# One stretch of small matmul tiles per turn: gated linear attention followed by a gated SSM on one core

## The chip, the cores and the metric

The kernel runs on one core of a Trainium2 chip. The metric is the device time of one execution in microseconds (us), as the median of several runs. TensorE is called PE below (PEld for its weight loads), VectorE DVE, ScalarE ACT, GpSimd POOL and SyncE SP, as in the profile.

## The reference

Two blocks follow each other, all in float32: attention with a recurrent state, gated per channel (4 batches, 8 heads, 768 steps, head size 48), and a gated state-space block (384 in, 512 inside, 384 out).

```python
for t in range(S):                                   # attention, per batch and head
    state = alpha[t][:, None] * state + outer(k[t], v[t])
    y[t] = q[t] @ state
x = y.transpose(0, 2, 1, 3).reshape(B, S, H * D)     # (4, 768, 384)

proj = x @ w_in                                      # (384, 1024)
val, gate = proj[..., :512], proj[..., 512:]
a = exp(A_log)[0]
for t in range(S):
    h = a * h + val[:, t];  ys[:, t] = h
out = (silu(gate) * ys) @ w_out                      # (512, 384)
```

## The kernel before

The 768 steps of a batch are cut into groups of 256 steps; there are N = 12 groups, numbered over the batches. A loop runs over n = 0 to 11. In turn n the kernel does the second block of group n and works ahead on the attention of the groups n+1 and n+2, and on the input of group n+3. The order of the instructions on every engine is the order of the program text (`manual_schedule`); each engine works through its own queue in that order and waits, by semaphores, for the others. So where a call stands in the loop decides what an instruction waits behind.

For a group m the steps are these.

- **products(m)**, seven steps on DVE, handed out one at a time by `go(count)`: transpose the raw alpha (`al`), transpose k, the running product P (a scan over 1028 elements), then ratio, reciprocal and the reverse scan V, then Zk = k * V, then transpose q, then Zq = q * P. The raw tiles `raw_a`, `raw_k`, `raw_q` come by DMA from SP's queue (`load_raw`), one buffer each.
- **scores(m)**: 64 matmuls on 64 x 64 tiles of PE (L798), Zk against Zq, into two pairs of PSUM banks, one pair for each half of the group.
- **masks(m)**: DVE multiplies half of the scores by a triangular mask into `A0` (L813), ACT copies the other half into `AK` (L814) and the keys into `K0` (L820), and POOL masks `AK` in place (L818).
- **values(m, across)** (L834): the masked scores times v, into the bank pair y. It is called twice, once for one diagonal (`across`), once for the other.
- **carried(m, us)** (L847): the state before each quarter of the group times Zq, into the same y.
- **states(m)** (L866): what each quarter adds to the state; ACT copies it to `dS` (L874), and **add_up(m)** lets POOL add it to the running `sum` tiles (L886).
- **join(m)**: ACT copies y to SBUF (L960, L961), SP and POOL issue four DMAs each that move the heads into place in xT (L963), and ACT copies the parts that stand in place already (`rest`, L966).
- **project(n, cc)**, four times per turn: twelve matmuls on the full 128 x 128 array (L988), six for the values into one bank (pv) and six for the gates into a second (pg); DVE scans pv (`hh`, L995), ACT makes silu of pg (L1006), POOL multiplies the two (L1008).
- **output_parts(n)**: the product with w_out as seven half-size products of sums (L1064, 28 matmuls on the full array) into four banks pa, pd, pc, pb. It is a generator with stops. ACT copies partial results (L1072), DVE adds them up (L1091, which reads pb; L1092, which reads pd; L1093, which reads pc), POOL adds the last quarter (L1089, L1094), and SP stores the rows (L1096). `sum_early` and `sum_late` (L1055 to L1060) make the sums of inputs.

PSUM has eight banks. Four (mm0 to mm3) are handed out by a string of digits, `taken`, one digit for each call of `bank()`; two (s0, s1) are for the scores and states, and two (y0, y1) for y. A bank is free again when the last engine that reads it is done.

In a turn of the middle part PE's order is: values(n+1, across) and states(n+1) are first, for which the scores were made in the turn before; then the four projections; then carried and the second values of group n+1; scores(n+2); the output products of group n; and the next turn begins. In the turns after n = 1 and 3 (`late`) scores, values and states stand elsewhere: after the output products, and between the projections. So PE goes to and fro between small and full tiles several times per turn.

While the kernel runs, it also tests whether the inputs lie in the range that this fast path can compute (`check_w`, `check_end`, `check_flag`); the flag is loaded by all engines near the end, and a branch takes a slower general path if it is not set. With the inputs of the reference the fast path's last part runs (L1373).

Of the kernel before, what the change touches and what calls it, by code (L numbers as in the profile page):

```python
# [9 lines left out]
FP32 = mybir.dt.float32  # L10
# [3 lines left out]
AF = mybir.ActivationFunctionType  # L14
# [332 lines left out]
def fast(  # L347
# [22 lines left out]
    nc = tc.nc  # L370
# [104 lines left out]
    AK = const.tile([C, G, 4, D + L], FP32, name="AK")  # L475
    As, Ks = [A0, AK[:, :, :, D:]], [K0, AK[:, :, :, 0:L]]
    Zqs = [const.tile([C, 2 * G, 4, L + D], FP32, name=f"Zq{i}") for i in range(2)]
# [183 lines left out]
    def products(m):  # L661
# [20 lines left out]
    taken = iter("0321032103231023" "1023102310231023" "102310231023" "10"  # L682
                 "23012301" "230132" "02130213" "023101" "23012301" "230132" "01230123" "012310"
                 "23012301" "230132" "01230123" "012310" "23012301" "230132" "01230123" "012310"
                 "23012301" "0132" "01320132")

    def bank(tag=None):
        if tag:
            return ps_at.tile([C, 512], FP32, tag=tag, name=tag)
        return ps_mm.tile([C, 512], FP32, tag=f"mm{next(taken)}", name="mm")  # L690

# [109 lines left out]

    def masks(m, cs=range(G), between=None):
        sc = [[t[:, 0:4 * (L + D)].rearrange("p (h x) -> p h x", h=4) for t in pair] for pair in scs[m]]
        mb = mask[:, None, :]
        if m < NG:
            for c in cs:
                for i in range(2):
                    nc.vector.tensor_mul(As[i][:, c], sc[c][i][:, :, D:], mb.to_broadcast([C, 4, L]))
                for i in range(2):
                    nc.scalar.activation((K0, dS[m % 2][1])[i][:, c, :, 0:D], sc[c][i][:, :, 0:D], AF.Copy)  # L810
            return
        for c in range(G):
            nc.vector.tensor_mul(A0[:, c], sc[c][0][:, :, D:], mb.to_broadcast([C, 4, L]))  # L813
            nc.scalar.activation(AK[:, c], sc[c][1], AF.Copy)  # L814
        if between:
            between()
        t = AK.rearrange("p c h x -> p (c h) x")[:, :, D:]
        nc.gpsimd.tensor_mul(t, t, mb.to_broadcast([C, G * 4, L]))  # L818
        for c in range(G):
            nc.scalar.activation(K0[:, c, :, 0:D], sc[c][0][:, :, 0:D], AF.Copy)  # L820

    def values(m, across):

        v_sb = vs[m % NV]
        if across:
            ys[m] = [t.rearrange("p (e t) -> p e t", e=2) for t in bank_pair("y")]
        for c in range(G):
            for e in range(2):
                for h in range(2):
                    i = 1 - h if across else h  # L830
                    for s in range(2):
                        p = 2 * e + (s ^ i)
                        rows = ds(L * h, L)
                        nc.tensor.matmul(ys[m][i][ds(64 * s, 64), e, ds(c * C + h * L, L)],  # L834
                                         v_sb[rows, c, 4 * i + p, :], As[i][rows, c, p, :],
                                         start=across and c == 0 and e == 0, stop=False, skip_group_check=True)
# [14 lines left out]
    def states(m):  # L851
# [7 lines left out]
        for c in range(G):  # L859
            for p in range(4):  # L860
                for h in range(2):
                    if c < n[h]:
                        rows = ds(L * h, L)
                        for i in range(2):
                            to = st[h][ds(64 * i, D), c, p, :] if m else st[h][c][ds(64 * i, D), p, :]
                            nc.tensor.matmul(to, ((K0, dS[m % 2][1]) if m < NG else Ks)[i][rows, c, p, 0:D],  # L866
                                             wide[rows, c, ds(2 * D * (4 * i + p), D)] if m == 0 else
# [199 lines left out]
    def output_parts(n):  # L1067
# [8 lines left out]
        product(pd, S3, T3, True)  # L1076
        yield
        copy(s7, pd)
# [96 lines left out]

    def second(m):
        if m < N:
            values(m, True)
            states(m)
            add_up(m, (0, 1, 2))  # L1180

    def third(m):
        if m < N:
            carried(m, (1,))
            values(m, False)
            carried(m, (0, 2, 3))
            return join(m, [nc.sync, nc.gpsimd])

    late = (1, 3)
    for n in range(N):  # L1190
# [37 lines left out]
        elif n == 1:  # L1228
# [28 lines left out]
            scaled_k(3, tk, V)  # L1257
            f2()
            output(0)
            sum_weights()  # L1260
# [4 lines left out]
            scaled_q(3, tq, P)  # L1265
            f3()
            go(1)
        else:
            if n == 2:
                first(m)  # L1270
            if n - 1 not in late:
                go(1)
                if n == N - 2:
                    check_w(5)
                next(outs, None)
                second(m)
                go(1)
                if n == N - 2:
                    check_w(0)
            else:  # L1280
                go(2 if n == 2 else 1)
            f0 = project(n, 0)
            f0()
            if n == N - 2:
                check_w(1)
            if n == 2:
# [8 lines left out]
            if n - 1 in late:  # L1295
                second(m)
            if n == 4:
                go(1)
            if n == N - 2:
                check_w(2)  # L1300
# [5 lines left out]
            go(1)  # L1306
            load_raw("q", n + 3, nc.sync)
            f3 = project(n, 3)
# [8 lines left out]
            if n < N - 1:  # L1317
                outs = output_parts(n)
            if n not in late and m + 1 < N:
                scores(m + 1)  # L1320
                masks(m + 1, between=lambda: next(outs))
                if m >= NG:
                    rest()
                    add_up(m, (3,))
                next(outs)
                go(1)
                if n == N - 3:
                    check_w(4)
            else:
                if m < N and m >= NG:  # L1330
                    rest()
                    add_up(m, (3,))
                if n < N - 2:
                    go(1)
                    for _ in outs:
                        pass
            load_v(m + 2, nc.sync)
        if n == N - 2:
            check_flag()
        if n == N - 1:  # L1340
            tc.mark_branch_hint_location("last", hint=0, engines=[mybir.EngineType.PE, mybir.EngineType.Activation, mybir.EngineType.DVE, mybir.EngineType.SP, mybir.EngineType.Pool])
            value = nc.values_load(flag[0:1, 0:1], min_val=0, max_val=1)
        if n == 1:
            output(n)
        if n == N - 2:
            for _ in outs:
                pass
        if n > 1 and n in late:
            first(m + 1)
# [62 lines left out]
```

## Time and profile before

| | |
|---|---|
| median of 3 runs | 274.02 us (273.98 to 274.11) |
| the profiled execution | 274.39 us, of which the span of instructions is 272.7 us |
| busy: PE / PEld / DVE / ACT / POOL | 265.9 / 230.3 / 234.7 / 111.5 / 161.6 us |
| granted PE clock | 0.999 |
| projections, L988 | 576 matmuls, 129.7 us |
| output products, L1064 | 252 matmuls (108 + 72 + 36 + 36), 51.7 us |
| DMA | 41.19 MB, mean 151 GB/s |

The page gives for each engine how long it was busy and how many instructions it had. A matmul of this kernel appears twice, as the load of the weights (PEld) and as the product (PE). In a timeline each row has the start in us from the beginning of the span, the length in us, the engine, the line, the operation, what it writes and reads, the shapes and the count of merged instructions; in brackets stands how long the engine was idle before it, and what ended that. A row of the windows has, for a stretch of time, its length and the busy time and instructions of PE, PEld, DVE, ACT and POOL, then the granted clock, the DMA engines' share and GB/s.

### The profile page before, as it was taken

What the parts mean: (1) busy time and instruction counts of PE and PEld (TensorE: products, weight loads), DVE (VectorE), ACT (ScalarE), POOL (GpSimd) and SP (SyncE); (2) the same over time, 40 slices, a digit from 0 to 9 for tenths busy, and PEclk for the clock granted to TensorE, in tenths of its full rate; (3) what the DMA queues carried; (4) which work ended last, traced back from release to release, by engine and by line L of the source; (5) the groups of instructions that cost most, each with busy time, mean ns of one, the idle gap of its engine ahead of it and who ended that gap; (6) DMA issues with size and microseconds to landing.
All of it is one profiled execution on the core that took longest, in us unless ns stands there. A gap on an engine that the chain in (4) does not pass through costs nothing.

```text
span 272.7 us, 9967 instructions
## 1 busy us (share of the span) xinstructions
PE 265.9 (97%) x4168; PEld 230.3 (84%) x4168; DVE 234.7 (86%) x316; ACT 111.5 (41%) x270; POOL 161.6 (59%) x185
## 2 busy tenths in 40 slices
PE   8999999999998999999999999999999999999995
PEld 6988888877786888888988988988988889888874
DVE  6979998996899999699999998999998998882430
ACT  3767766462341631441542433524525515214111
POOL 8122323175116997689985995996876976646000
PEclk9999999999999999999999999999999999999999
DMA  6937984998692669396588479595587501201101
GB/s 185 308 123 239 295 188 154 241 194 208 195 219 72 139 158 226 94 232 160 113 213 174 103 193 196 118 242 143 138 206 158 139 2 31 75 0 46 60 7 58
DMA packets 52304, 41.19 MB, mean 151 GB/s; under 512 B 27392, under 2 KB 50944, under 8 KB 52256
## 3 DMA queue, kind: packets, MB, share of 16 engines
q1 hardware_dynamic: 49328, 37.34, 55.2%
q0 software_dynamic: 1536, 2.20, 3.0%
q10 hardware_dynamic: 1392, 0.99, 1.2%
q8 instruction: 34, 0.56, 0.9%
q14 instruction: 14, 0.11, 0.2%
HBM read 32.54 MB, written 4.72 MB: 137 GB/s over the span
## 4 chain that ended last, share of the span: by engine, by line
PE 82%; DVE 10%; issue 2%; ACT 2%; DMA 1%; POOL 1%; DVEq 0%; ACTq 0%; POOLq 0%
PE mm L988 42%; PE mm L1064 15%; PE y L834 4%; PE y L847 4%; PE mm L1022 4%; PE mm L798 3%; PE s L798 3%; PE s L866 3%; DVE P L635 2%; PE mm L1373 2%; DVE V L654 2%; PE mm L707 1%; DMA raw_a<-in_alpha_dram 1%; DVE hh L995 1%; DVE k L600 1%
## 5 line engine op out<-in xcount | busy, mean ns | idle before, releaser
L988 PE MATMUL mm<-xT,w_in 128*128 128x256 f32 x576 | 129.7, 382 | 0.8 <-DVE hh L995 0.7
L988 PEld LDWEIGHTS mm<-xT,w_in 128*128 128x128 f32 x576 | 107.8, 190 | 16.9 <-DVE hh L995 1.1
L1006 ACT ACTIVATE sg<-mm 128x256 f32<-128x256 f32 x48 | 18.4, 384 | 89.2 <-PE mm L988 84.2
L1008 POOL TENSOR_TENSOR f_last<-sg,hh 128x256 f32<-128x256 f32 x36 | 30.2, 845 | 30.6 <-ACT sg L1006 21.7
L886 POOL TENSOR_TENSOR sum<-sum,dS 128x192 f32<-128x192 f32 x30 | 38.3, 1276 | 3.7 <-ACT dS L874 2.3
L635 DVE TENSOR_TENSOR_SCAN P<-al,lower 128x1028 f32<-128x1028 f32 x12 | 30.1, 2510 | 0.3
L995 DVE TENSOR_TENSOR_SCAN hh<-a_dec,hh,mm 128x256 f32<-128x256 f32 x32 | 23.4, 730 | 8.0 <-PE mm L988 7.7
L654 DVE TENSOR_TENSOR_SCAN V<-al,ends 128x1028 f32<-128x1028 f32 x12 | 29.3, 2439 | 0.4
L963 POOL DMA_DIRECT2D xT<-yst x44 | 22.5, 516 | 4.6 <-ACT yst L960 3.2
L556 POOL TENSOR_TENSOR w_in<-w_in,wr 128x768 int32<-128x768 int32 x4 | 7.3, 1823 | 25.9 <-DVE wr L551 16.1
L1064 PE MATMUL mm<-wide,wr 128*128 128x192 f32 x108 | 20.5, 326 | 0.0
L600 DVE STREAM_TRANSPOSE k<-raw_k 128x1024 f32<-128x1024 f32 x9 | 18.4, 2049 | 0.0
L600 DVE STREAM_TRANSPOSE q<-raw_q 128x1024 f32<-128x1024 f32 x9 | 18.2, 2025 | 0.0
L1064 PEld LDWEIGHTS mm<-wide,wr 128*128 128x128 f32 x108 | 18.0, 190 | 0.0
L818 POOL TENSOR_TENSOR AK<-AK,mask 128x512 f32<-128x512 f32 x9 | 13.4, 1494 | 7.7 <-ACT AK L814 7.6
L874 ACT ACTIVATE dS<-s 128x384 f32<-128x384 f32 (+1 forms) x18 | 7.4, 461 | 23.8 <-PE s L866 23.8
L619 DVE TENSOR_TENSOR Zk<-k,V 128x1024 f32<-128x1024 f32 (+1 forms) x14 | 16.5, 1181 | 0.1
L600 DVE STREAM_TRANSPOSE al<-raw_a 128x1024 f32<-128x1024 f32 x8 | 16.4, 2051 | 0.0
L1064 PE MATMUL mm<-w_out,f_last 128*128 128x192 f32 x72 | 15.8, 342 | 0.1
L610 DVE TENSOR_TENSOR Zq<-q,P 128x1024 f32<-128x1024 f32 (+1 forms) x14 | 15.2, 1087 | 0.0
L847 PEld LDWEIGHTS y<-Zq,sum 48*64 48x64 f32 x656 | 11.7, 134 | 3.9 <-issue 2.5
L834 PEld LDWEIGHTS y<-AK,v 64*64 64x64 f32 x352 | 12.1, 134 | 2.9 <-issue 2.9
(188 smaller groups left out, 503.4 us busy)
## 6 DMA issues: line engine op xcount, KB each, us to landing
v<-in_v_dram SPq DMA_DIRECT2D x22, 192.0 KB, 3.3
out_dram<-o_sb SPq DMA_DIRECT2D x22, 192.0 KB, 2.7
raw_k<-in_k_dram SPq DMA_DIRECT2D x18, 184.0 KB, 4.7
raw_q<-in_q_dram SPq DMA_DIRECT2D x18, 184.0 KB, 4.3
raw_k<-in_k_dram SPq DMA_DIRECT2D x18, 176.0 KB, 5.0
raw_q<-in_q_dram SPq DMA_DIRECT2D x18, 176.0 KB, 4.7
wbits<-in_moe_w_in_dram SPq DMA_DIRECT2D x8, 384.0 KB, 5.4
raw_a<-in_alpha_dram SPq DMA_DIRECT2D x16, 184.0 KB, 3.9
```

What stands on the lines that cost most here:

```text
L600: nc.vector.transpose(out=by_runs(to).rearrange("p h c j -> p h j c"), in_=raws[name][:, 0:4 * ROW].rearrange("p (h j d) -> p h j d", h=4, ...
L635: nc.vector.tensor_tensor_scan(out=P, data0=al[:, 0:4 * GP], data1=lower.rearrange("p h t -> p (h t)"), initial=0.0, op0=ALU.mult, op1=ALU ...
L654: nc.vector.tensor_tensor_scan(out=V[:, ::-1], data0=al[:, 1:4 * GP + 1][:, ::-1], data1=ends.rearrange("p h t -> p (h t)")[:, ::-1], init ...
L834: nc.tensor.matmul(ys[m][i][ds(64 * s, 64), e, ds(c * C + h * L, L)], v_sb[rows, c, 4 * i + p, :], As[i][rows, c, p, :], start=across and ...
L847: nc.tensor.matmul(ys[m][i][ds(64 * s, 64), e, ds(u * L, L)], Ss[j][rows, p, :], Zqs[m % 2][rows, u, p, D:], start=False, stop=True, skip_ ...
L886: nc.gpsimd.tensor_add(Ss[j][:, :, 0:D], Ss[j - 1][:, :, 0:D], part)
L963: engines[n % len(engines)].dma_start(out=xT[to, a], in_=st[rows, i, e])
L988: nc.tensor.matmul((pv, pg)[vg], w_ins[cc][:, kk, vg, :], xT[:, kk, :], start=(kk == 0), stop=(kk == NK - 1))
L995: nc.vector.tensor_tensor_scan(out=hh, data0=a_dec[:, cc:cc + 1].to_broadcast([C, GC]), data1=pv, initial=prev_h[cc][:, GC - 1:GC] if n % ...
L1006: nc.scalar.activation(sg, pg, AF.Silu)
L1008: f = lambda: engine.tensor_mul(fs[n][cc], sg, hh)
L1064: nc.tensor.matmul(o, a[:, k], b[k] if type(b) is list else b[:, k], start=start and k == 0, stop=k == KC - 1, skip_group_check=True)
```

## The change

The order of one turn is rewritten. From n = 3 on, all small tiles of a turn stand in one place: after the four projections come scores(n+2), carried and the second values of group n+1, states(n+2) and the first values of group n+2; then all seven output products of group n; then the next turn's projections. The additions of the output (L1091 to L1094 of the old numbering, and the store) stay in the next turn, but come after one more step of `go`, behind V. The four state additions of POOL come after the output products instead of being split. Because scores(n+2) now come before the second values of group n+1, the masked scores of two groups live at once: `A0` and `AK` get a second buffer, taken from the raw bits of w_out, which are checked earlier for that (`check_w(4)`, now at n = 1). POOL masks in two operations of half the size. The y of group n+2 is written before that of group n+1 has been read, so y and the output products take turns in the banks y0, y1 and mm0 to mm3 (the letters a and b in the string). The flag is loaded before the last projection.

```diff
+    spare_A = wobits[0].rearrange("p a n two -> p (a n two)").bitcast(FP32)
+    AKs = [spare_A[:, 0:G * 4 * (D + L)]..., AK]
+    A0s = [spare_A[:, ds(G * 4 * (D + L), G * 4 * L)]..., A0]
...
-                 "23012301" "230132" "01230123" "012310" "23012301" "230132" "01230123" "012310"
-                 "23012301" "0132" "01320132")
+                 "23012301" "23" "01" "23ba" "23ab23ab" "23" "ab" "2310"
+                 "23012301" "23" "01" "23ba" "23ab23ab" "23" "ab" "2310"
+                 "23012301" "2310" "23ab01ab")
...
         for c in range(G):
-            nc.vector.tensor_mul(A0[:, c], sc[c][0][:, :, D:], mb.to_broadcast([C, 4, L]))
-            nc.scalar.activation(AK[:, c], sc[c][1], AF.Copy)
-        if between:
-            between()
-        t = AK.rearrange("p c h x -> p (c h) x")[:, :, D:]
-        nc.gpsimd.tensor_mul(t, t, mb.to_broadcast([C, G * 4, L]))
-        for c in range(G):
+            nc.vector.tensor_mul(A0s[m % 2][:, c], sc[c][0][:, :, D:], mb.to_broadcast([C, 4, L]))
+            nc.scalar.activation(AKs[m % 2][:, c], sc[c][1], AF.Copy)
             nc.scalar.activation(K0[:, c, :, 0:D], sc[c][0][:, :, 0:D], AF.Copy)
+            t = AKs[m % 2][:, c, :, D:]
+            nc.gpsimd.tensor_mul(t, t, mb.to_broadcast([C, 4, L]))
...
         product(pd, S3, T3, True)
-        yield
         copy(s7, pd)
...
         else:
+            go(1)
-            if n - 1 not in late:
-                go(1)
-                next(outs, None)
-                second(m)
-                go(1)
+            if n > 2:
+                go(1)
+                next(outs, None)
             f0 = project(n, 0)
             f0()
...
             f3 = project(n, 3)
             f3()
             if m + 1 < N:
                 go(1)
+                scores(m + 1)
+                masks(m + 1)
...
-            rest = third(m)
-            if n < N - 1:
-                outs = output_parts(n)
-            if n not in late and m + 1 < N:
-                scores(m + 1)
-                masks(m + 1, between=lambda: next(outs))
-                if m >= NG:
-                    rest()
-                    add_up(m, (3,))
-                next(outs)
-                go(1)
+            if m < N:
+                sum_late()
+                carried(m, (1,))
+                values(m, False)
+                carried(m, (0, 2, 3))
+                rest = join(m, [nc.sync, nc.gpsimd])
+            if m + 1 < N:
+                states(m + 1)
+                values(m + 1, True)
+            if m < N:
+                rest()
+                outs = output_parts(n)
+                next(outs)
+            if m + 1 < N:
+                add_up(m + 1)
+                go(1)
```

More of the change, by code (lines that the diff above doesn't have):

```diff
@@ L800, in scores, with masks @@
                                          start=True, stop=True, skip_group_check=True)
-    def masks(m, cs=range(G), between=None):
+    def masks(m, cs=range(G)):
         sc = [[t[:, 0:4 * (L + D)].rearrange("p (h x) -> p h x", h=4) for t in pair] for pair in scs[m]]
@@ L1174, in first @@
             masks(m)
[L1176 to L1180, printed above, removed]
-    def third(m):
[L1183 to L1189, printed above, removed]
+    def third(m):
+        carried(m, (1,))
+        values(m, False)
+        carried(m, (0, 2, 3))
+        join(m, [nc.sync, nc.gpsimd])
     for n in range(N):
@@ L1258, in fast @@
             f2()
+            check_w(4)
             output(0)
@@ L1294, in fast @@
                 sum_early()
-            if n - 1 in late:
-                second(m)
-            if n == 4:
+            if n == 2:
                 go(1)
+                values(m, True)
+                states(m)
+                add_up(m)
             if n == N - 2:
@@ L1307, in fast @@
             load_raw("q", n + 3, nc.sync)
+            if n == N - 1:
+                tc.mark_branch_hint_location("last", hint=0, engines=[mybir.EngineType.PE, mybir.EngineType.Activation, mybir.EngineType.DVE, mybir.EngineType.SP, mybir.EngineType.Pool])
+                value = nc.values_load(flag[0:1, 0:1], min_val=0, max_val=1)
             f3 = project(n, 3)
```

64 lines of the change are left out of this document (28 added, 36 removed), and 2 rows, old and new, of the table taken.

## The prediction

> **What bounds the kernel now.** I read the page first, then the windows of whole turns, then the timelines of single engines inside one turn.
>
> ```profile
> span 272.7 us, 9967 instructions
> PE 265.9 (97%) x4168; PEld 230.3 (84%) x4168; DVE 234.7 (86%) x316; ACT 111.5 (41%) x270; POOL 161.6 (59%) x185
> PEclk9999999999999999999999999999999999999999
> PE 82%; DVE 10%; issue 2%; ACT 2%; DMA 1%; POOL 1%; DVEq 0%; ACTq 0%; POOLq 0%
> 196.24:215.92 19.68, 19.68 (x324) 17.54 (x316) 18.78 (x23) 7.85 (x20) 15.15 (x17) 1.00 0.74 170
> sum 99.08, PE 99.08 PEld 88.35 DVE 94.23 ACT 39.09 POOL 77.10; mean PE 19.82 PEld 17.67 DVE 18.85 ACT 7.82 POOL 15.42
> ```
>
> PE leads, but the last two rows (five whole turns, from 136.74 to 235.82) matter more: in a mean turn of 19.82 us PE works all the time and DVE 18.85 us. So DVE has about 1 us per turn to spare, and its queue is in order. What a shorter PE turn is worth depends on where DVE stands when PE needs it. The profiled execution took 274.39 us, 1.7 over its span; the median of the runs is 274.02, so I sum on 274.39 and take 0.4 off at the end.
>
> **The merged small tiles.** In the turns from n=2 on, by the two orders of instructions, PE enters a stretch of small tiles (scores, values, carried, states) 20 times before and 11 times after: nine fewer.
>
> ```profile
> 96.38 10.63 PE L988 MATMUL mm<-xT,w_in 128*128 128x256 f32 x48
> 115.30 5.45 PE L988 MATMUL mm<-xT,w_in 128*128 128x256 f32 x24
> 215.92 10.63 PE L988 MATMUL mm<-xT,w_in 128*128 128x256 f32 x48
> 226.48 0.46 PE L847 MATMUL y<-Zq,sum 48*64 48x64 f32 x16
> 235.82 10.63 PE L988 MATMUL mm<-xT,w_in 128*128 128x256 f32 x48
> ```
>
> Two groups of 24 projections last 10.90 us, one of 48 lasts 10.63: 0.27 for cutting it once, on the side of the big tiles, of which part is an overlapping tail. With the small side I estimate 0.35 per merge (bounds 0.2 and 0.5). Nine make 3.2 us, and a turn of PE work falls from 19.92 ((235.82 - 96.38) / 7) to about 19.5. This is a gain only if nothing is late.
>
> **What it moves on DVE.** Here is turn 8 into turn 9.
>
> ```profile
> 205.61 0.74 DVE L995 TENSOR_TENSOR_SCAN hh<-a_dec,hh,mm 128x256 f32<-128x256 f32 x1 [0.72 <-PE mm L988]
> 206.27 2.04 DVE L600 STREAM_TRANSPOSE al<-raw_a 128x1024 f32<-128x1024 f32 x1
> ...
> 208.65 0.83 DVE L1060 TENSOR_TENSOR wr<-f_last,wr 128x256 f32<-128x256 f32 x1
> ...
> 212.01 2.69 DVE L635 TENSOR_TENSOR_SCAN P<-al,lower 128x1028 f32<-128x1028 f32 x1
> 214.62 0.32 DVE L1091 TENSOR_TENSOR wr<-wide,mm 128x192 f32<-128x192 f32 x1
> 214.98 0.35 DVE L1092 TENSOR_TENSOR o_sb<-wr,mm 128x192 f32<-128x192 f32 x1
> 215.25 0.34 DVE L1093 TENSOR_TENSOR o_sb<-wr,mm 128x192 f32<-128x192 f32 x1
> 215.51 0.15 DVE L651 TENSOR_TENSOR ratio<-P,ends 128x4 f32<-128x4 f32 x1
> 215.70 0.18 DVE L652 RECIPROCAL ends<-P 128x4 f32<-128x4 f32 x1
> 215.92 2.54 DVE L654 TENSOR_TENSOR_SCAN V<-al,ends 128x1028 f32<-128x1028 f32 x1
> 218.38 0.65 DVE L995 TENSOR_TENSOR_SCAN hh<-a_dec,mm 128x256 f32<-128x256 f32 x1
> ```
>
> The output adds (L1091 to L1093) read the product banks. The second, L1092, frees the bank `pd`, and by the string of banks that bank is the gate bank of the next turn's first projection. PE needs it 6/48 of the way into the projections: 215.92 + 1.32 = 217.24. L1092 ends at 215.33, so there are 1.9 us to spare. In the changed order of instructions the adds of turns 3 to 9 stand behind ratio, reciprocal and V: 218.38 - 215.51 = 2.87 us later on DVE. With PE 0.35 earlier, 1.9 becomes -1.3: the first gate matmuls wait, and all of PE's work is queued behind them.
>
> That wait closes a loop. From the end of L1092 (call it R) to PE's restart:
>
> ```profile
> 82.87 0.74 DVE L995 TENSOR_TENSOR_SCAN hh<-a_dec,hh,mm 128x256 f32<-128x256 f32 x1
> 83.67 1.13 PE L988 MATMUL mm<-xT,w_in 128*128 128x256 f32 x4 [0.65 <-DVE hh L995]
> ```
>
> 0.06 (83.61 to 83.67). Then 36 of the 48 instructions up to the end of the fourth value pass: 36/48 of 10.56 (215.92 to 226.48) is 7.92. DVE starts the fourth scan 0.13 later (205.61 against 196.24 + 42/48 of the same 10.56). From that scan to the next, DVE takes 12.77 (205.61 to 218.38); L1093 falls behind R, which with the tail of L1092 makes 12.6 to the next R. Loop: 0.06 + 7.92 + 0.13 + 12.6 = **20.7 us**, against 19.92 now. The masks' two operations move ahead of L1059, which is no change in their sum. A new wait within PE (the third product now goes into a y bank that ScalarE must first empty, an estimated 0.3) is hidden by the 1.2 us of stall; without the stall it costs its 0.3.
>
> **What it moves on GpSimd and SyncE.** After the products GpSimd now does three or four adds of states (L886) *ahead* of the output add L1094, and SyncE, also in order, sends the output rows, which wait for L1094, ahead of the next `raw_a`.
>
> ```profile
> 157.09 2.26 POOL L886 TENSOR_TENSOR sum<-sum,dS 128x192 f32<-128x192 f32 x1 [0.29 <-ACT dS L874]
> 161.19 0.59 POOL L886 TENSOR_TENSOR sum<-sum,dS 128x192 f32<-128x192 f32 x1
> 209.18 2.04 POOL L963 DMA_DIRECT2D xT<-yst  x4
> 156.49 2.13 SPq L1096 DMA_DIRECT2D out_dram<-o_sb  x2
> 158.68 1.86 SPq L411 DMA_DIRECT2D raw_a<-in_alpha_dram  x4
> DMA to landing us min/median/max: 3.0/3.5/4.0
> DMA to landing us min/median/max: 3.0/3.8/4.5
> ```
>
> An add takes 0.59 when DVE leaves it alone and 2.26 when it meets V: it ends when V does. So the adds begin at V's end, R - 0.7. Two or three fit before the product Zk, 1.5 us later; the rest waits for Zk. With 0.67 from add to add (0.59 and a gap) and an estimated 1.2 for Zk, L1094 then ends at about R + 3.5 with four adds and R + 2.9 with three (bounds: R + 2.6 without any meeting, R + 4.5). The output issue adds 0.45. The last two rows are the landings of the `raw_a` of 158.68 and of 137.57: the fourth is issued 1.43 after the first and lands 4.0 or 4.5 later, so 5.4 to 5.9; I take 5.7. `raw_a` is there at R + 9.65 or R + 9.05. DVE wants it after the fourth scan, R + 8.11 + 0.66 = 8.77. It is late by 0.9 or 0.3, and the loop is 21.6 or 21.0. Of the six loops from turn 3 to turn 9, four have four adds: 4 x 21.6 + 2 x 21.0 = 128.4 us.
>
> **The sum.** The start, around n=1 and n=2:
>
> ```profile
> 65.40 0.75 DVE L995 TENSOR_TENSOR_SCAN hh<-a_dec,hh,mm 128x256 f32<-128x256 f32 x1 [2.47 <-PE mm L988]
> 72.79 0.42 DVE L813 TENSOR_TENSOR A<-s,mask 128x256 f32<-128x256 f32 x1 [0.96 <-PE s L798]
> 73.56 0.42 DVE L813 TENSOR_TENSOR A<-mm,mask 128x256 f32<-128x256 f32 x1 [0.34 <-PE mm L798]
> 87.27 0.73 DVE L995 TENSOR_TENSOR_SCAN hh<-a_dec,hh,mm 128x256 f32<-128x256 f32 x1
> L567 DVE TENSOR_REDUCE wmin<-wbits 128x1 f32<-128x768 f32 x4 | 3.8, 944 | 0.0
> L1366 PEldq COMPARE_BRANCH  x1: 3708/3708/3708, 260.0 to 260.0; - x1
> ```
>
> check_w(4), two reductions of 0.94, fits into the 2.47 of idle time. A transpose moved ahead fills the 0.96 + 0.34, so the fourth scan of n=2 comes 1.1 earlier (bounds 0.6 and 1.3, by how far P meets the masks on GpSimd): 86.2. Plus 12.6: R of turn 3 at 98.8, where before the same matmul started at 96.38 + 1.32 = 97.70. Then 98.8 + 128.4 = 227.2 for turn 9, before 217.24: **+10.0 us**. From there turn 9 has one merge (-0.35) and the y-bank wait (+0.3); in turns 10 and 11 DVE has no transposes or scans of new groups any more, and the reductions put there fill their place. Loading the flag earlier is worth nothing: PE's branch itself waits 3.7 us for PE's queue to run out. 274.39 + 10.0 - 0.4 = **284.0 us**.
>
> **Rivals.**
> *The loads are in time.* If L1094 or the landings are 0.9 quicker, six loops of 20.7 make 124.2 and the sum 279.8 (278 to 281). For it: the landing times spread by more than this. 0.22.
> *Faster: DVE keeps up.* It decides at a chain of 19.5 - 8.11 = 11.4 us from the fourth scan to L1092. If GpSimd no longer meets L1060 (0.83 here), P (2.69) and V (2.54), an estimated 0.4 + 0.4 + 0.3 less, the 12.6 come down to 11.5, PE does not wait, and the nine merges give 274.0 - 3.2 = 270.8. Against it: GpSimd has the same 15.4 us of work per turn, and four adds now queue behind P and V. 0.14.
> *Part of the stall only*, 274 to 278: chains between 11.4 and 12.2. 0.09.
> *The xT copies slip under a scan.* GpSimd's four DMA issues (2.04) come 1.6 us later than before, next to P. If P holds them for its 2.3, xT lands about 2 us late, 0.6 behind the stall, and the case with loads in time becomes 283.4; with late loads P begins after them and nothing is added. No row shows an issue during a scan. [...] 0.05.
> *Worse, 289 and more*, by loads that land over a microsecond later or a lower PE clock in the stalls of 1 to 2.3 us: 0.05. The one stall shown (0.65 at 83.67) left the clock at 9 tenths or more. [...]
>
> **Numbers.** The forecast has 0.45, with a range of its own of 281 to 288 (0.5 per loop). 0.2% (0.5 us) is about what a measurement of this kernel tells from no change. Faster: 0.14. Within 0.2%: 0.02, out of the partial case. Slower: 0.45 + 0.22 + 0.07 + 0.05 + 0.05 = 0.84. The range of 275 to 289 leaves out the faster case, the top 0.04 and the lowest edge of the partial one.
>
> **What would show it.** Right: in turns 3 to 9 PE's seventh L1001 projection instruction waits 1 to 2 us for DVE's output add, turns of 21 to 21.6 us, DVE's transpose of `al` waits for the landing of `raw_a`, one stretch of small tiles per turn. Wrong: turns near 19.5 without such a wait (DVE kept up), or a stall of 1.2 without a wait of `al` (loads in time), or a wait for xT ahead of the first projection.

## The result and the profile after

The changed kernel takes 292.57 us (median; 290.61 to 294.92) against 274.0 for the kernel before: a ratio of 1.068, with a 95% interval of 1.059 to 1.078. That is slower, as forecast, but outside the range of 275 to 289. The profiled execution took 294.92 us, 20.5 more than that of before.

These are lines of its page, of the windows of five whole turns (columns as in the prediction's window rows: length, busy time and count of PE, PEld, DVE, ACT and POOL, granted clock, DMA share, GB/s), and of the list of waits (total, times, longest).

```profile
span 292.9 us, 9976 instructions
PE 272.1 (93%) x4168; PEld 240.2 (82%) x4168; DVE 233.2 (80%) x316; ACT 112.5 (38%) x270; POOL 137.6 (47%) x194
PEclk9999999999999999996997998899599999999999
PE 72%; issue 8%; DVE 7%; DMA 5%; SPq 3%; POOL 2%; ACT 2%; ACTq 0%; DVEq 0%; POOLq 0%
188.56:214.52 25.96, 22.55 (x334) 20.60 (x333) 18.85 (x21) 7.98 (x20) 11.06 (x18) 0.87 0.57 129
235.65:256.55 20.90, 19.74 (x318) 18.03 (x317) 14.72 (x21) 6.73 (x18) 13.65 (x22) 1.00 0.12 35
sum 113.96, PE 104.05 PEld 95.20 DVE 89.77 ACT 38.86 POOL 58.29; mean PE 20.81 PEld 19.04 DVE 17.95 ACT 7.77 POOL 11.66
...
DVE wr L1103 <- PE mm L1077: 7.8, 3, 4.6
PE s L879 <- issue: 6.7, 4, 2.3
DVE wr L1103 <- PE y L1077: 5.5, 2, 3.6
PE mm L860 <- issue: 5.0, 3, 2.1
PE y L847 <- issue: 2.5, 2, 1.3
```

A turn takes 113.96 / 5 = 22.8 us instead of 19.82, and in these turns no other engine holds PE up for more than 0.3 us at a time: DVE waits for PE's products (7.8 + 5.5), not PE for DVE. PE stands still 14.2 us (6.7 + 5.0 + 2.5) with the releaser "issue", that is, with nothing shown that it waits for. And the same 4168 matmuls keep it busy for 6.2 us longer, with a clock row that is no longer all nines.

Here is one such stop in PE's timeline, and the clock around it in the windows:

```profile
131.53 0.20 PE L879 MATMUL s<-v,wobits 64*48 64x48 f32 x1
134.05 0.31 PE L879 MATMUL s<-v,K 64*48 64x48 f32 x1 [2.32 <-issue]
...
128.09:133.60 5.51, 3.65 (x206) 3.52 (x205) 5.43 (x7) 3.00 (x7) 4.35 (x7) 1.00 0.67 144
133.60:140.40 6.80, 6.35 (x66) 6.23 (x67) 4.87 (x6) 2.49 (x7) 0.83 (x3) 0.50 0.43 92
...
135.57:142.59 7.02, 7.02 (x28) 6.89 (x28) 0.65 0.29 56
231.00:235.65 4.65, 4.65 (x28) 4.52 (x28) 1.00 0.58 122
```

PE stops in the middle of states(m+1), between two matmuls of one kind, and then runs 6.8 us at half clock. The last two rows are the 28 output products (L1077) of that turn and of an undisturbed one: 7.02 against 4.65.

**What the stops have in common** appears when all of PE's records (matmuls, weight loads and what its sequencer does itself, above all 104 waits on semaphores) are numbered in the order in which they start. Counted without the waits, the stops show no common place. This is a list from the trace's records, not a view of the profile:

```
stop at us (length)   PE instruction   modulo 256
 89.48 (0.91)          3266            194
108.90 (1.39)          3778            194
131.53 (2.52)          4546            194
155.52 (1.92)          5058            194
179.06 (2.21)          5825            193
201.48 (2.34)          6338            194
205.73 (1.60)          6594            194
228.05 (1.84)          7105            193
250.26 (1.38)          7874            194
```

All nine stand at one place modulo 256 (193 where a product's record starts 1 to 2 ns ahead of its weight load's). The DMA queue q8, of kind instruction, moves packets of 16,384 bytes: 34 of them in this execution, in which PE has 8446 records, 33.0 times 256. So I read the stretches from one such place to the next as blocks of instructions that PE gets with one packet each, and as windows they show the limit (the same block in the kernel before stands last):

```profile
129.78:134.05 4.27, 1.96 (x143) 1.83 (x134) 4.19 (x6) 2.07 (x5) 4.02 (x7) 0.95 0.48 109
198.49:203.82 5.33, 3.21 (x129) 2.74 (x127) 5.25 (x7) 1.91 (x5) 3.07 (x4) 1.00 0.52 105
248.33:251.64 3.31, 2.15 (x142) 2.01 (x134) 3.27 (x7) 2.70 (x8) 3.05 (x6) 1.00 0.11 30
sum 32.93, PE 19.53 PEld 17.74 DVE 31.98 ACT 17.62 POOL 23.69; mean PE 2.44 PEld 2.22 DVE 4.00 ACT 2.20 POOL 2.96
...
147.31:149.59 2.28, 2.28 (x129) 2.28 (x132) 2.25 (x3) 1.18 (x3) 1.59 (x2) 1.00 0.49 101
```

The sum is over eight such blocks: 4.12 us each, of which PE works 2.44. In the kernel before a block of small tiles passed in 2.28 us without a stop: there the small tiles of a turn come as 144 or 160 and as 80 or 96 matmuls, with 5 us of products between them, and the block behind was there in time (its fetch began at 145.88). The change puts 240 or 256 small matmuls, with their weight loads about two blocks of instructions, in one piece. In the first of the windows above, the boundary at 129.78, the packet starts at 131.42, ends at 132.63, and PE goes on at 134.05. What stood ahead of it can be read in the DMA strip of the same stretch (40 slices of 0.107 us, busy tenths):

```profile
DMA  9999999999864338110000000000000664621285
q8 instruction: 1, 0.02, 1.8%
```

For the first 1.1 us (10 slices) the engines are full of loads; the fetch comes as they run out.

**The account** of +20.5 between the two profiled executions. Stops: the nine lengths add up to 16.1, less a usual step of 0.03 each, 15.8. One wait for L1104: 0.7. Merging: projections 10.45 against 10.56 between first starts, products 4.65 against 4.92, 0.38 per turn and 3.4 for nine. The early flag: -0.6 (by the profiled executions of number 7 below; 0.2 by its medians). The rest is 20.5 - 15.8 - 0.7 + 3.4 + 0.6 = 8.0, and I put it down to the half clock: the four product groups that ran in it show 5.6 of that (7.02 + 4.87 + 5.48 + 6.79 - 4 x 4.65), and the other 2.4 was not measured by itself.

### The profile page after: what moved, and what is told of

It is laid out like the page before. It is cut to its first block, busy times and chain, and to the rows that moved or that the text cites. A ratio compares the mean times of both kernels' runs of the same rounds, so it can differ in the third digit from the quotient of the medians.

```text
span 292.9 us, 9976 instructions
## 1 busy us (share of the span) xinstructions
PE 272.1 (93%) x4168; PEld 240.2 (82%) x4168; DVE 233.2 (80%) x316; ACT 112.5 (38%) x270; POOL 137.6 (47%) x194
## 4 chain that ended last, share of the span: by engine, by line
PE 72%; issue 8%; DVE 7%; DMA 5%; SPq 3%; POOL 2%; ACT 2%; ACTq 0%; DVEq 0%; POOLq 0%
PE mm L1001 28%; PE mm L1077 11%; PE y L1001 7%; DMA raw_k<-in_k_dram 4%; PE mm L1035 4%; PE s L879 3%; PE s L814 3%; PE y L1077 2%; PE y L847 2%; PE mm L814 2%; SPq L411 2%; PE y L860 2%; DMA raw_q<-in_q_dram 2%; PE mm L1367 2%; DVE P L646 2%
## 5 line engine op out<-in xcount | busy, mean ns | idle before, releaser
L1001 PE MATMUL mm<-xT,w_in 128*128 128x256 f32 x456 | 103.7, 382 | 0.8 <-DVE o_sb L1104 0.7
L1001 PEld LDWEIGHTS mm<-xT,w_in 128*128 128x128 f32 x456 | 85.7, 190 | 13.2 <-DVE o_sb L1104 1.1
L1019 ACT ACTIVATE sg<-mm 128x256 f32<-128x256 f32 x38 | 14.6, 383 | 85.6 <-PE mm L1001 85.6
L1001 PE MATMUL y<-xT,w_in 128*128 128x256 f32 x120 | 27.5, 380 | 0.0
L1008 DVE TENSOR_TENSOR_SCAN hh<-a_dec,hh,mm 128x256 f32<-128x256 f32 x26 | 19.3, 741 | 8.7 <-PE mm L1001 8.4
L1001 PEld LDWEIGHTS y<-xT,w_in 128*128 128x128 f32 x120 | 22.9, 190 | 3.1
L899 POOL TENSOR_TENSOR sum<-sum,dS 128x192 f32<-128x192 f32 x30 | 22.7, 757 | 1.9
L1101 POOL TENSOR_TENSOR wide_S<-wide_S,wr 128x192 f32<-128x192 f32 x9 | 8.9, 985 | 24.7 <-ACT wr L1085 24.7
L567 POOL TENSOR_TENSOR w_in<-w_in,wr 128x768 int32<-128x768 int32 x4 | 7.3, 1823 | 25.4 <-DVE wr L562 16.1
L1077 PE MATMUL mm<-w_out,f_last 128*128 128x192 f32 x72 | 18.7, 390 | 0.1
L879 PE MATMUL s<-v,K 64*48 64x48 f32 x320 | 12.2, 217 | 7.0 <-issue 6.7
L1077 PE MATMUL mm<-wide,wr 128*128 128x192 f32 x76 | 16.8, 361 | 0.0
L1077 PEld LDWEIGHTS mm<-w_out,f_last 128*128 128x128 f32 x72 | 14.3, 228 | 1.2 <-ACT wide L1085 0.4
```

Of the source, the lines that this page charges most:

```text
L879: nc.tensor.matmul(to, K_of(m)[i][rows, c, p, 0:D], wide[rows, c, ds(2 * D * (4 * i + p), D)] if m == 0 else vs[m % NV][rows, c, 4 * i + p ...
L899: nc.gpsimd.tensor_add(Ss[j][:, :, 0:D], Ss[j - 1][:, :, 0:D], part)
L1001: nc.tensor.matmul((pv, pg)[vg], w_ins[cc][:, kk, vg, :], xT[:, kk, :], start=(kk == 0), stop=(kk == NK - 1))
L1008: nc.vector.tensor_tensor_scan(out=hh, data0=a_dec[:, cc:cc + 1].to_broadcast([C, GC]), data1=pv, initial=prev_h[cc][:, GC - 1:GC] if n % ...
L1077: nc.tensor.matmul(o, a[:, k], b[k] if type(b) is list else b[:, k], start=start and k == 0, stop=k == KC - 1, skip_group_check=True)
```

## The experiments

T1 is the theory above. T2: the stops are a wait for data that the profile doesn't name. T3: the prediction's chain of late output adds and late loads makes the loss.

**1. Move the block boundaries.** 32 tiny matmuls more in the warm-up (the trace shows each call as two matmuls and two weight loads, so 128 PE instructions):

```diff
+    keep_warm(32, 16)
```

> The changed kernel with 32 more tiny matmuls (128 more PE instructions) in its warm-up. Theory T1: PE runs dry of instructions. Its instructions come in blocks of 256 by DMA (16,384 bytes on the queue of kind instruction), and the merged small tiles use a block up in about 2 us where the next takes 3.3 to 5.3 us to come. By T1 the stops of 0.9 to 2.5 us that the trace of the changed kernel shows with the releaser issue stay at the same place modulo 256 in the stream of all PE instructions, so that each stands 128 instructions earlier in the kernel's own order: stops at kernel-own numbers 3266 - 128 and so on (or + 128 where the next boundary is the one that lies in the stretch), at other lines of the small tiles than now. Rival T2: a hidden wait for data (the masks of the next group, K0 or A0, or a bank) that the profile does not name: the same matmuls as now stop (kernel-own numbers 3266, 3778, 4546, 5058, 5825, 6338, 6594, 7105, 7874). Time: 285 to 296 by either.

Measured: 312.15 us. Seven stops of 1.3 to 4.5 us, at instructions 3266, 4034, 4546, 5314, 5826, 6593 and 7362 of the stream, all again 193 or 194 modulo 256. In the kernel's own order (128 less) they are 128 (give or take one) before or behind the stops above, and none is at its old matmul. T2 falls. The time was missed: the warm-up matmuls took 13.9 us themselves (16.74 instead of 2.85), and from the first products of turn 2 on both kernels take 202 us.

**2. Small tiles that wait for nothing**, 512 calls (2048 PE instructions) at the start of the kernel before:

```diff
+    def train(n):
+        t, z = bank_pair("y"), nc.const_aps.tensor(0.0, [C, C], FP32)
+        for j in range(n):
+            i, s = j % 2, j // 2 % 2
+            nc.tensor.matmul(t[i][ds(64 * s, 64), 0:64], z[ds(64 * i, 64), 0:64], z[ds(64 * i, 64), 0:64], ...)
...
     keep_warm(3, 256)
+    train(512)
```

> The kernel before with 512 matmuls of 64x64 tiles (about 2048 PE instructions, weight loads among them) that wait for nothing, at the start, behind the warm-up. Their results go to banks that are not read. T1: after what is already at hand, each block of 256 instructions takes 3.3 to 5.3 us, with a stop at the boundary whose releaser is issue: 2048 instructions take 24 to 40 us. T2 (no limit on instructions): 256 of them take about 2.1 us, as in the merged stretch of the changed kernel where it does not stop, so 17 us in all without stops over 0.3 us. If the clock follows stops, the granted clock falls to 0.5 in this stretch by T1 and not by T2.

Measured: 303.28 us. The blocks as windows:

```profile
6.30:11.97 5.67, 2.25 (x141) 2.11 (x134) 0.00 (x0) 0.00 (x0) 1.77 (x2) 1.00 0.98 298
11.97:16.28 4.31, 2.09 (x129) 1.96 (x129) 0.00 (x0) 0.00 (x0) 0.00 (x0) 1.00 0.57 179
16.28:20.03 3.75, 3.30 (x129) 3.11 (x129) 0.00 (x0) 0.00 (x0) 0.00 (x0) 0.57 0.01 4
23.50:26.98 3.48, 2.09 (x128) 1.95 (x129) 0.00 (x0) 0.00 (x0) 0.00 (x0) 1.00 0.02 5
26.98:30.46 3.48, 2.10 (x129) 1.96 (x130) 0.00 (x0) 0.00 (x0) 0.00 (x0) 1.00 0.02 5
```

PE needs 2.1 us for a block and gets one every 3.48 when nothing else moves: the packet starts 1.1 behind the boundary, lasts 0.93, and the next block runs 1.4 after its end. With the DMA engines at 0.98 it was 5.67. Shown: a limit of PE's own supply, with a part that depends on other transfers. Four blocks in a row took 3.47 or 3.48. The third row has the half clock that began behind the second stop.

**3. The products put back between the small tiles** (the string of banks is adapted to it):

```diff
-            if m + 1 < N:
-                states(m + 1)
-                values(m + 1, True)
             if m < N:
                 rest()
                 outs = output_parts(n)
                 next(outs)
             if m + 1 < N:
+                values(m + 1, True)
+                states(m + 1)
                 add_up(m + 1)
```

> The changed kernel with the output products put back between the small tiles: scores, carried, values, then the products, then values and states of the next group (which go to the y banks, as in the changed kernel). The output adds stay behind V, the loads and adds of states where the change puts them. T1: blocks of instructions are used up no faster than in the kernel before; no PE wait of over 0.5 us with the releaser issue from turn 3 on, the granted clock stays at 0.97 or more, and the time falls from 292.6 to what the chain of output adds leaves: 277 to 284. T3 (the prediction's chain by itself: output adds behind V, late raw_a, makes all of the loss): 290 or more, with PE's waits on the output adds. T2: the waits with releaser issue go on, at the next group's values or states, 288 to 293.

Measured: 287.86 us (284.88 to 290.41). In the profiled execution, the slowest of the four (290.41), there are three stops of over 2 us instead of nine stops, of 2.1, 3.7 and 3.0 us, each at a boundary in the long stretch of small tiles. T1's forecast of none was wrong, and its time (277 to 284) with it: a shorter stretch isn't enough when the fetch starts late, and here it started 1.8, 4.1 and 3.5 us behind the boundary before, with a DMA share of 1.0.

**4. The prediction's second step by itself**, in the kernel before:

```diff
-                next(outs, None)
                 second(m)
                 go(1)
+                next(outs, None)
```

> The kernel before with one step moved: the output adds (DVE's three, GpSimd's one) issue behind ratio, reciprocal and V instead of ahead of them. Nothing is merged. The prediction's second step by itself: R (end of the add that frees bank pd) 2.87 us later on DVE, PE stalls 0.9 per turn and the loop is 20.6 to 21.4 against 19.92: 6 or 7 loops, +4 to +9, 278 to 283. If DVE has more slack than that (T1 alone explains the changed kernel's loss): 274 to 276. No stop with the releaser issue over 0.5 us by either.

Measured: 284.17 us (283.11 to 285.88); ratio 1.036 (1.031 to 1.042). Waits, DVE's timeline and a window from one restart of PE to the next:

```profile
PE mm L988 <- DVE o_sb L1092: 5.3, 5, 1.3
PE mm L988 <- DVE wr L1091: 2.2, 1, 2.2
...
182.36 2.30 DVE L654 TENSOR_TENSOR_SCAN V<-al,ends 128x1028 f32<-128x1028 f32 x1
185.44 0.35 DVE L1092 TENSOR_TENSOR o_sb<-wr,mm 128x192 f32<-128x192 f32 x1
...
164.70:185.85 21.15, 20.17 (x316) 17.67 (x316) 19.28 (x23) 7.69 (x20) 16.25 (x18) 1.00 0.72 158
```

The prediction's wait, at its place: PE's gate projection waits for L1092 behind V, and the loop is 20.96 to 21.23 us (forecast 20.7 without late loads). No stop on "issue" over 0.3 in the turns. So T3's mechanism is real, and worth 10 us where nothing else stops PE; 1.2 above the line's upper bound, where one stop of 2.2 was followed by 3.4 us at half clock.

**5. The same adds put back early in the changed kernel:**

```diff
-                go(1)
                 next(outs, None)
+                go(1)
```

> The changed kernel with the output adds issued ahead of ratio, reciprocal and V again, so that the prediction's second step is undone and the merged stretch of 256 small matmuls stays. T1 (blocks of 256 instructions run out inside the stretch, the granted clock halves behind the longer stops): about nine stops of 0.9 to 2.5 us with the releaser issue remain, all at the same place modulo 256, and the time is 284 to 291. T3 (the chain of late output adds makes the loss by itself): PE keeps going, the merges show as a gain, 270.8 to 274.

Measured: 293.24 us (292.75 to 296.06). No gain at all, and 2.2 above T1's line. The nine stops remain, at the same instructions, of 1.1 to 4.1 us, and DVE waits still longer for PE (16.7 + 14.2 us). T3 doesn't explain the changed kernel: while PE starves, DVE has the time.

**6. Both undone: products between, adds early on DVE** (the diffs of 3 and 5 together).

> Both undone: the output products stand between the small tiles, and the output adds ahead of V. What stays of the change is one shape of turn, the start around n=1 and n=2, the masks in two buffers, the rotating y banks and the early flag. In the kernel with the products between and the adds late, three stops of 2.1 to 3.7 us remained, each at a boundary whose fetch began 1.8 to 4.1 us after the boundary before it, while the DMA engines were full of raw_a, raw_k and raw_q; those loads were late because SyncE sends them behind the output rows. T1: with the adds early the loads come some 3 us sooner, the fetches find the DMA engines less full and no stop of over 1 us remains: 271.5 to 275. If the fetches still queue behind loads: 277 to 284 with stops of 2 us and more. T3 alone would give 271.5 to 275 as well, but with no fetch stop in either kernel.

Measured: 286.03 us (284.32 to 286.92): the second outcome by its stops, 2.0 above its line by the time. Stops of 1.9, 2.5 and 1.9 us at three boundaries remain, and four of 1.1 to 2.3 in the products, on GpSimd's sum L1068. SyncE's output rows, begun at 138.63, waited for GpSimd's add, so that raw_a was issued at 145.19, 5.9 us behind the start of the turn's projections (139.32); in the kernel before it is issued 0.8 us behind that start in the same turn (137.57 and 136.74). The trace thus named the next suspect, GpSimd's order.

**7. The flag early, alone**, in the kernel before (the two lines of the flag moved ahead of the last turn's fourth projection):

> The kernel before with one step moved: the flag is loaded, and the branch hinted, ahead of the last turn's fourth projection instead of at its end. The prediction's step: worth nothing, 274.0 to 274.2, since PE's branch waits for PE's queue to run out. Rival: the branch takes a fixed 3.4 to 3.7 us from the moment that the flag is read (the instructions behind it are fetched in that time), so it is begun earlier beside the last projections, and the gap of 0.6 us between the last projection and the first matmul behind the branch goes: 273.3 to 273.6.

Measured: 273.62 us against 273.81 (ratio 0.998, 0.996 to 0.999). The branch begins earlier and still lasts 3.8 us; it ends when the last projection does, and the 0.44 us of issue before L1373 is gone:

```profile
L1366 PEldq COMPARE_BRANCH  x1: 3832/3832/3832, 259.3 to 259.3; - x1
...
263.91 1.53 PE L1373 MATMUL mm<-w_out,f_last 128*128 128x384 f32 x4 [0.44 <-issue]
...
263.33 1.85 PE L1373 MATMUL mm<-w_out,f_last 128*128 128x384 f32 x5
```

The second row is the kernel before, the third this one. It is a small gain, and the only kernel here that beats the one before.

**8 and 9. GpSimd's order undone too**, with the products between (8) and with the merged stretch (9): add_up behind next(outs), sum_late ahead of the scores, output adds early on DVE.

```diff
                 next(outs, None)
+                if m < N:
+                    add_up(m)
                 go(1)
...
+            if m < N:
+                sum_late()
             if m + 1 < N:
                 scores(m + 1)
                 masks(m + 1)
...
-                sum_late()
                 carried(m, (1,))
...
-                add_up(m + 1)
```

> The kernel with the products between the small tiles and the adds early on DVE, with GpSimd's order undone too: the output add ahead of the four adds of states, and the sums for the next products (sum_late) issued ahead of the scores and masks. In the kernel without this step SyncE's output rows waited 6.5 us for GpSimd's output add, raw_a was issued 7 us later than in the kernel before, DVE waited 10.5 us in all for raw_a, and PE 5.8 us in all for the sum S1. If the late loads are also what filled the DMA engines when PE's instructions were due: no stop of over 1 us on releaser issue, no wait for S1, and 271.5 to 275. If stretches of 160 and 112 matmuls are too much for the fetch in any case: 277 to 283 with stops of about 2 us at every third boundary.

> The changed kernel with the same three undone (output adds ahead of V on DVE, output add ahead of the adds of states on GpSimd, sums ahead of the masks), so that of the loss only the merged stretch of 256 small matmuls is left. T1: the second boundary in the stretch comes at the earliest 3.3 to 3.5 us behind the first, where PE would need it after 1.9: eight or nine stops of at least 1.1 us, longer where loads are in flight, and half clock for some us behind those of about 2 us and more: 283 to 291. If T1's stops were only there because late loads were in the way: 271 to 277.

Measured: 281.99 us (281.33 to 283.27) and 284.6 (283.9 to 286.41). In number 9 the merged stretch stays, with the three orders undone. It has five stops at boundaries, of 1.3 to 2.4 us, where the line had eight or nine; none is followed by half clock in the profile, and it is 8.6 us faster than number 5, which differs only in GpSimd's order and the place of sum_late. A second cost appears that the longer stops had covered: states(m+1) comes so soon after its scores that PE waits for ScalarE's copy of K (the waits: 4.5 us, 5 times). Number 8 has the time of its second outcome, but not the stops of about 2 us: those at boundaries are down to 1.4, 1.1 and 0.8. The evictions of the new scores now stand ahead of the products' copies on ScalarE, and PE waits 4.6 us in all for those.

**10. The small tiles of 2 with one load repeated nine times:**

```diff
-    load_steps("q", 1, [nc.sync])
+    for _ in range(9):
+        load_steps("q", 1, [nc.sync])
```

> The kernel before with 512 matmuls of 64x64 tiles at the start that wait for nothing, as in the earlier run of that kind, and with one load (raw_q of the second group) issued nine times in place of once, so that the DMA engines stay full for the whole of them. In the earlier run a block of 256 instructions took 5.67 us with a DMA share of 0.98, 4.31 with 0.57, and 3.48 five times over with 0.02. If the block queues behind data: 4.3 to 7 us per block as long as the loads last, in the stretches that took 3.48. If a fetch takes a fixed time: 3.48 again. The time of the whole says nothing, since later loads are pushed back.

Measured: 306.0 us. Behind the first block the loads came in bursts, with shares of 0.34 to 0.60 and not full. Blocks took 5.88, 4.86, 4.30, 3.47, 3.48, 3.47 and 4.03 (the line above says that 3.48 had come five times; it was four). Inconclusive: with shares of 0.39 to 0.50 three blocks took 3.47 and 3.48, as with quiet engines.

**11. Take the load out of the way, in number 9:**

```diff
-            load_raw("q", n + 3, nc.sync)
             if n == N - 1:
...
+            load_raw("q", n + 3, nc.sync)
             load_v(m + 2, nc.sync)
```

> The merged kernel with the chain undone (284.6 us), and with the load of raw_q moved from ahead of the fourth projection to behind the output products, so that no load of 1.4 MB is in flight when PE goes into the merged stretch; raw_q is wanted some 10 us after that, by DVE's transpose. In the kernel without this step the fetches that decide the stops began 0.5 to 1.6 us behind their boundary with the DMA engines full, and the next boundary came 3.1 to 4.2 us behind it. If the fetch queues behind the load: they begin 0.5 to 1.1 behind, the next boundary comes 3.1 to 3.5 behind, the stops shrink by about 0.5 us each, and the time is 280 to 283. If the fetch takes its time whatever the DMA engines do: 284 to 286, or more where raw_q comes late.

Measured: 281.21 us (280.99 to 281.6), as T1 said (raw_q is 0.72 MB, not the 1.4 of the line above). Eight blocks of the merged stretches, in number 9 and then here, with the sums over all eight:

```profile
129.74:133.25 3.51, 2.36 (x143) 1.98 (x134) 3.48 (x6) 1.51 (x5) 1.96 (x3) 1.00 0.28 55
sum 30.32, PE 19.41 PEld 17.70 DVE 29.99 ACT 14.54 POOL 19.71; mean PE 2.43 PEld 2.21 DVE 3.75 ACT 1.82 POOL 2.46
...
128.71:131.93 3.22, 2.15 (x142) 1.89 (x137) 3.19 (x6) 1.21 (x4) 1.67 (x3) 1.00 0.05 9
sum 26.49, PE 19.20 PEld 17.59 DVE 26.29 ACT 11.91 POOL 17.09; mean PE 2.40 PEld 2.20 DVE 3.29 ACT 1.49 POOL 2.14
```

PE works as long on them in both (19.4 and 19.2), and in the changed kernel (19.5, above); only the time that the blocks take shrinks, from 32.9 over 30.3 to 26.5 in all. Moving one load, with no instruction of PE's changed, gave 3.4 us: loads in flight delay the fetches. Not every block shows it: one took 3.66 and then 3.67 although its DMA share fell from 0.28 to 0.01, and there PE waits 1.2 us for ScalarE's copy of K in both. What is left, 3.3 us per block, is near the 3.48 of number 2.

**12. GpSimd's output add alone put back**, in the changed kernel (the add_up part of 9):

> The changed kernel (292.6 us) with one of the three undone alone: GpSimd's output add goes ahead of the four adds of states again. DVE's output adds stay behind V, the sums for the next products stay behind the masks. Undoing DVE's part alone had brought nothing (293.2), all three 284.6. If the late output rows, and through them the late loads that lie in the way of the fetches and make the longer stops and the half clock, come from GpSimd's order: 285 to 289, with raw_a issued within 3 us of the first projection's start. If both orders must be undone for it: 290 to 294.

Measured: 289.79 us (288.64 to 293.49), between the two outcomes, and in the profiled execution, the slowest, its stops are no shorter than the changed kernel's (1.4 to 3.7). How the 8.0 us from the changed kernel to number 9 divide between GpSimd's order, the place of sum_late and DVE's adds stays open: neither DVE's adds (number 5) nor GpSimd's add alone brings them, and the place of sum_late was not run alone.

## Why the prediction was wrong, point by point

**The direction was right, for a reason that hardly came into play.** The step that failed is the first, the merged small tiles: I priced a merge by what switching costs and added "a gain only if nothing is late", but looked for lateness on the other engines and in the data, not in PE's own instructions. As a price of the arithmetic the step was right: 0.38 per merge (forecast 0.35), and the turn at 235.65 without its stop would be 20.90 - 1.34 = 19.56 (19.5). The missing term is 15.8 us of stops and some 8 of half clock.

**The wait for bank pd** was right as a mechanism and by size (number 4), and hidden in the changed kernel but once:

```profile
106.51 2.08 DVE L611 STREAM_TRANSPOSE al<-raw_a 128x1024 f32<-128x1024 f32 x1 [0.81 <-DMA raw_a<-in_alpha_dram]
118.35 0.35 DVE L1104 TENSOR_TENSOR o_sb<-wr,mm 128x192 f32<-128x192 f32 x1
118.76 0.48 PE L1001 MATMUL mm<-xT,w_in 128*128 128x256 f32 x1 [0.69 <-DVE o_sb L1104]
164.91 0.35 DVE L1103 TENSOR_TENSOR wr<-wide,mm 128x192 f32<-128x192 f32 x1 [1.36 <-PE mm L1077]
```

The first three rows are the predicted chain, in turns 3 and 4: raw_a late by 0.81 (forecast 0.9), then PE waiting for L1104. The fourth is what every later turn shows: DVE waits for PE. That number 4 gives the forecast's +10.0 is partly chance, since it has only one late raw_a (0.9 in all its waits) and adds a stretch of half clock.

**GpSimd and SyncE.** In turn 3 output rows and loads were late as worked out: SyncE's output rows waited 3.8 us, and raw_a was issued at 100.72, where R + 3.95 is 100.49. In turns 4 to 8 the rows took 1.2 us at most, and DVE waited for raw_a no more, since PE stood still. The price that the runs show isn't DVE's wait. It is that loads in flight delay PE's fetches (3.4 us for one load, number 11).

**The y-bank wait** isn't seen: the products run in 4.65 where the kernel before has 4.92.

**The start** was better than forecast: the fourth scan of n=2 at 85.02 (86.2), and L1104 of turn 3 ends at 96.54 (98.8), since that chain took 11.5 us and not 12.6: GpSimd met DVE less, as the rival "DVE keeps up" had it: P took 2.23 us and V 2.30, where the prediction's rows have 2.69 and 2.54. Later chains took up to 12.6 without their waits, so that rival's condition held in part.

**The xT copies under a scan**: the prediction says that no row shows an issue of GpSimd during a scan. The kernel before has such rows: of the four issues from 57.67, the last three run beside V's scan (58.39 to 60.69). The changed kernel has many. Each takes 0.50 to 0.54 us there as elsewhere, and PE never waits for xT. So that rival's outcome isn't seen where scans and issues meet.

**The flag**: "worth nothing" was wrong. PE's branch takes 3.4 to 3.8 us in seven of the kernels here, the one before, the changed one and number 7 among them, but 1.1 to 2.0 in numbers 2, 3, 6 and 8, and only 0.4 in numbers 1, 9 and 11. These rows are the changed kernel's and number 9's:

```profile
L1360 PEldq COMPARE_BRANCH  x1: 3392/3392/3392, 280.4 to 280.4; - x1
...
L1363 PEldq COMPARE_BRANCH  x1: 395/395/395, 269.8 to 269.8; - x1
```

The branch did not wait for PE's queue to run out; begun earlier, it ends under the last projections. What it waits for can be read beside the packets of q8: in the changed kernel one starts at 281.43 and ends at 282.38, and the branch ends at 283.78, 1.4 later, about as PE goes on at a block boundary. So it is in all eleven kernels in which a packet ends during the branch or just before it; in the three of 0.4 us there is none. PE's branch, too, waited for a block of instructions.

**The rival "worse, 289 and more"** had 0.05 and named the lower clock, but behind stalls of another origin. I hadn't weighed PE's own supply of instructions. In the kernel before PE passes the block boundaries ahead of the branch without a stop of over 0.3 us; two blocks of small tiles in a row don't pass so, at 3.48 us per block against 2.1 (number 2).

## What to carry to other kernels

Count instructions, not only microseconds: in these runs a stretch in which PE passed 256 instructions in much less than 3.5 us (2.1 to 2.3) lived on what had been fetched before it, and a second such block in a row stopped it (number 2 got a block every 3.48 us), so small tiles belong between large matmuls, as in the kernel before. That kernel already shows it to whoever looks, in the instruction queue's packets and in blocks of 2.1 to 2.3 us. When stops show the releaser "issue" between two like matmuls, number the engine's records, semaphore waits included, and see what the DMA engines carry at that time: here one load moved by some us was worth 3.4 us. And a wait that is worth 10 us alone may be worth nothing beside another one: undo both before you judge either.

## What the runs showed of the hardware that was not expected

At every stop at a block boundary, in all runs, PE went on 1.2 to 1.7 us after the end of the instruction packet (1.24 to 1.49 at the changed kernel's nine). At these stops the packet started 0.5 to 1.7 us (1.2 in the mean) after the boundary before it where the DMA engines' share until then was under 0.1, and 0.5 to 4.3 us (2.2 in the mean) where it was 0.9 or more.

In the changed kernel the granted clock fell to 0.50 four times, for 6.83, 3.41, 3.41 and 6.83 us, from 133.60, 157.49, 181.38 and 205.28 on. The stops that came ahead were of 2.52, 1.92, 2.21 and 2.34 us, and the lower clock began at times from 0.45 us before PE went on to 1.46 after. Behind the other five, of 0.91 to 1.84, it did not fall, nor behind one of 2.35 in number 9 or one of 3.6 in number 2. No stop under 1.7 was followed by it in any run.
